# Splitting x of the first block part by part among the last steps of the first attention groups

## The chip, the cores and the metric

The kernel runs on one core of a Trainium2 chip. The metric is the time of one execution on the device, in microseconds (us). The engines are TensorE (PE: matmuls, and PEld: its weight loads), VectorE (DVE), ScalarE (ACT), GpSimd (POOL) and SyncE (SP), which issues the transfers.

## The reference

```
attention: q, k, v of (4, 8, 576, 64); causal, window of 64 keys
  scores = q k^T / sqrt(64), masked; softmax; times v
x = attention as (2304, 512)
FFN 1: g = x w_gate;  x1 = (silu(g) * (x w_val)) w_out      d_ff 1536
FFN 2: h = x1 w_in;   out = (h * clip(h + 3, 0, 6) / 6) w_out2   d_ff 2048
```

All arrays are float32 and are computed to about that precision: each matmul operand is split into a rounded upper part (`hi`) and the rest (`lo`), and a product is three matmuls, hi x hi, lo x hi and hi x lo.

## The kernel before, in words

The 2304 tokens are cut into blocks of 512, 512, 512, 384 and 384. Attention works in 36 groups of 256 tokens and two heads; `x` of a block of 512 tokens needs eight of them (two token groups by four head pairs). `x` is kept as four parts of 128 rows, `xr[:, kc]`, where part kc belongs to head pair kc.

`first_block()` (L506) computes the first eight groups alone, as nothing else can run yet. It is a pipeline written out by hand, one loop step s per group and six more to drain it: at step s it loads q and k of group s + 2 and `v` of group s - 1, stores the result of group s - 5 into `xr` (`store_x`, on ScalarE here), copies the transposed probabilities of group s - 4 out of PSUM (`evac_t`, L460, ScalarE for odd groups, VectorE for even ones), runs the two halves of the softmax for groups s - 1 and s - 2, then the matmuls: scores of group s (L403), transposes of group s - 3 (L452), values of group s - 4 (L471). At the end `pump(CONVERT_ATTENTION[s])` runs that many operations of the weight conversion.

The conversion `w_ops()` (L115) turns float64 weights into float32 on chip: per tile L129 and L134 (ScalarE), L148, L151, L186 and L192 (VectorE) rebuild the number, then L183 (ScalarE) takes the upper part and L199 (VectorE) the rest. A raw tile is loaded (L107) when L192 of an earlier one has been issued; five raw tiles are held. Tiles 3c, 3c + 1 and 3c + 2 are the gate, value and output weights of chunk c.

After `first_block`, `split_x` (L328) takes apart the four parts of `xr`: a cast on ScalarE into `xh` (L331) and a subtraction on VectorE into `xl` (L332). Then come 36 steps (block t, chunk c) of FFN 1, n = 0 to 35: the gate product (`gate`, L541 to L543, 12 matmuls of 128 x 512), tanh (L576) and L577 on it, the value product, L584, the split of the result (L564, L569) and the output product of the step before (L591 to L593). The groups of the next blocks and further conversion run among them.

What sets the order: inside a `tc.manual_schedule()` each engine runs its instructions in the order of the program. `first_block` is one such block of code, step n = 0 is another, and steps from n = 24 on a third. `split_x` and steps 1 to 23 stand outside of them; there a planner with a model of the chip's time orders each engine's instructions, and it also interleaves those with the ordered blocks and these with each other. In the trace, for example, ScalarE runs two conversion operations of step 0 ahead of the store of group 7.

`up` is the pool that holds `xh`, `xl` (four tags each), `u`, `uh` and `ul`; it is opened after `first_block` has closed its own pool `at`. Later code takes tiles of the tags `xh*` and `xl*` for other things (`wide_tile`, `ob` in `store_out`).

Of the kernel before, what the change touches and what calls it, by code (L numbers as in the profile page):

```python
# [11 lines left out]
F32 = mybir.dt.float32  # L12
F32R = mybir.dt.float32r
# [10 lines left out]
DM = H * D  # L24
# [4 lines left out]
KC = DM // 128  # L29
TB = 512  # L30
# [39 lines left out]
def attention_two_ffn(ctx: ExitStack, tc, qk, qq, v, w, out):  # L70
# [19 lines left out]
    def psum(tag, bufs=1):  # L90
        return ps.tile([128, 512], F32, tag=tag, name=tag, bufs=bufs)
# [17 lines left out]
    def load_ahead(n):  # L109

        while len(w_loaded) <= n + (4 if len(w_loaded) < NW1 else 3):
            w_loaded.append(len(w_loaded))
            w_load(w_loaded[-1])
# [101 lines left out]
    def pump(k):  # L215

        for _ in range(k):
            next(w_iter, None)
# [99 lines left out]
    xhl = {}  # L318

    def new_x():  # L320
        return xp.tile([128, KC, TB], F32, tag="xr", name="xr")
# [3 lines left out]
        nc.sync.dma_start(out=t[:, :, :src.shape[-1]], in_=src)  # L325
        return t

    def split_x(xr, kc, size):  # L328
        hi = up.tile([128, TB], F32R, tag=f"xh{kc}", name="xh", bufs=1)[:, :size]
        lo = up.tile([128, TB], F32R, tag=f"xl{kc}", name="xl", bufs=1)[:, :size]  # L330
        nc.scalar.copy(hi, xr[:, kc, :size])  # L331
        nc.vector.tensor_tensor(  # L332
            out=lo, in0=xr[:, kc, :size], in1=hi.bitcast(F32), op=ALU.subtract
        )
        xhl[kc] = (hi, lo)

# [3 lines left out]
    per_block = TB // GT * NPAIR  # L342
# [3 lines left out]
    def masks():  # L346
        nc.gpsimd.memset(mask, 0.0)
        for h in range(2):
            a = mask[64 * h:64 * h + 64, 0, :]
            nc.gpsimd.affine_select(  # L350
                out=a, in_=a, compare_op=ALU.is_ge, fill=MASKED / SCALE,
                base=-1, pattern=[[1, 128]], channel_multiplier=-1,
            )
            nc.gpsimd.affine_select(
                out=a, in_=a, compare_op=ALU.is_ge, fill=MASKED / SCALE,
                base=WIN, pattern=[[-1, 128]], channel_multiplier=1,
            )
        nc.gpsimd.memset(mask[0:64, 1, 0:64], MASKED / SCALE)
        nc.gpsimd.tensor_copy(mask[64:128, 1, 0:64], mask[64:128, 0, 0:64])
        nc.vector.tensor_copy(mask[:, 1, 64:128], mask[:, 0, 64:128])  # L360
        make_identity(nc, ident)

    def open_attention(stack, bufs):
        pool = stack.enter_context(tc.tile_pool(name="at", bufs=bufs["s"], side="right", reuse_waits="tile"))
        a_pool[:] = [pool, bufs]
# [30 lines left out]
    def quarter_scores(n, s):  # L396

        t = a_held.pop((n, "qk"))
        for u in range(GB):
            for h in range(2):  # L400
                rows = slice(h * D, (h + 1) * D)
                k0 = GT + u * WIN
                nc.tensor.matmul(  # L403
                    s[h][u % 2 * WIN:(u % 2 + 1) * WIN, u // 2 * 128:(u // 2 + 1) * 128],
                    t[rows, u * WIN:(u + 1) * WIN], t[rows, k0:k0 + 128],
                    start=True, stop=True,
                )
        a_held[n, "s"] = s
# [91 lines left out]
    def within(lo, hi):  # L500
        def at(fn, n, *more):
            if lo <= n < hi:
                fn(n, *more)
        return at

    def first_block():  # L506

        xr = new_x()
        with ExitStack() as st:
            bufs = {"qk": 3, "v": 4, "y": 4, "pt": 2, "s": 4, "xg": 0}  # L510
            open_attention(st, bufs)
            at = within(0, per_block)
            at(load_qk, 0)
            load_ahead(-4)
            at(load_qk, 1)
            load_ahead(1 - 4)
            masks()
            for s in range(per_block + 6):
                at(load_qk, s + 2)
                at(load_v, s - 1)  # L520
                if s in FIRST_LOADS:
                    load_ahead(2 + FIRST_LOADS.index(s) - 4)
                at(store_x, s - 5, xr)
                at(evac_t, s - 4)
                at(softmax_a, s - 1)
                at(softmax_b, s - 2)
                if s < per_block:
                    quarter_scores(s, [psum("acc", 4) for _ in "ab"] if s % 2 else [psum("g"), psum("c")])
                at(transposes, s - 3, "vd"[s % 2])
                at(values, s - 4, "acc", 4)  # L530
                pump(CONVERT_ATTENTION[s])
        return xr
# [29 lines left out]
    def u_hi(u):  # L562
        hi = up.tile([128, TB], F32R, tag="uh", name="uh")[:, :u.shape[-1]]
        nc.scalar.copy(hi, u)  # L564
        return hi
# [111 lines left out]
            )  # L677

    def wide_tile(k):
        return up.tile([128, TB], F32, tag=f"x{'hl'[k % 2]}{k // 2}", name="hw", bufs=1)  # L680

    sums = {}

    def wide_sums(c):
# [3 lines left out]
        if c == 0:  # L688
            t = new_x()
            fa, fb = t[:, 0, :], t[:, 1, :]  # L690
        else:
            fa, fb = wide_tile(6), wide_tile(7)
# [28 lines left out]
    def wide_chunk(c, out, between):  # L721
# [5 lines left out]
        def copy(k, a):  # L727
            t = wide_tile(k)[:, :TW]
            nc.scalar.copy(t, a)
            return t  # L730

        def plus(k, a, b):
            t = wide_tile(k)[:, :TW]
            nc.vector.tensor_tensor(out=t, in0=a, in1=b, op=ALU.add)
            return t
# [161 lines left out]
    def store_out(k):  # L897

        for a, r0 in done[:k]:
            n = r0 // 128 % 6  # L900
            ob = up.tile([128, DM], F32, tag=f"x{'hl'[n % 2]}{n // 2}", name="ob", bufs=1)
            if r0 == NT - 128:
                for h, q in enumerate((nc.sync, nc.scalar)):
                    half = slice(h * DM // 2, (h + 1) * DM // 2)
                    if h:
                        nc.scalar.activation(ob[:, half], a[:, half], AF.Copy, scale=1.0 / 6.0)
                    else:
                        nc.vector.tensor_scalar(
                            ob[:, half], a[:, half], 1.0 / 6.0, None, op0=ALU.mult
                        )  # L910
                    q.dma_start(out=out[r0:r0 + 128, half], in_=ob[:, half])
                continue
            if n % 2 and r0 >= NT - 2 * TH:
                nc.vector.tensor_scalar(ob, a, 1.0 / 6.0, None, op0=ALU.mult)
            else:
                nc.scalar.activation(ob, a, AF.Copy, scale=1.0 / 6.0)
            nc.sync.dma_start(out=out[r0:r0 + 128, :], in_=ob)
        del done[:k]
# [39 lines left out]
    def unit(i, before, others):  # L958
# [9 lines left out]
        if i == 0:  # L968
            for k in range(2):
                for _ in swish(ORDER[k], h[ORDER[k]]):  # L970
                    pass
            for k in range(2):
                split_g(ORDER[k], i)
            before()
            rest.append(chain(*(swish(k, h[k]) for k in ORDER[2:])))
        else:
            if i == 1:
                for k in ORDER[2:]:
                    split_g(k, 0)
            for m, name in enumerate(ORDER):  # L980
                ffn2_out(name, i - 1)
                if m % 2:
                    store_out(3)
                if m in (1, 2):
                    advance(others, 1)
                if now:
                    if m:
                        split_g(ORDER[m - 1], i)
                    for _ in swish(name, h[name]):
                        pass  # L990
            if now:
                rest.append(one(split_g, ORDER[-1], i))
# [14 lines left out]
            next(it, None)  # L1007

    with ExitStack() as fixed:
        with tc.manual_schedule():  # L1010
            xr = first_block()
        up = ctx.enter_context(tc.tile_pool(name="up", bufs=2, reuse_waits="tile"))
        for kc in range(KC):
            split_x(xr, kc, TB)
        st = ExitStack()
        open_attention(st, {"qk": 1, "v": 1, "y": 2, "pt": 1, "s": 3, "xg": 2})
        start = ExitStack()
# [2 lines left out]
        for n, (t, c) in enumerate(steps1):  # L1020
# [8 lines left out]
            def at(fn, step, *more):  # L1029
                if step in group_at:  # L1030
                    fn(group_at[step], *more)

            pumps = CONVERT[t] if t + 1 < NB or c < CONVERT_STOP else 0
            if t + 1 < NB and c == 1:
                xr = new_x()
# [8 lines left out]
            if last and t + 1 < NB:  # L1044
                for kc in range(KC):
                    split_x(xr, kc, SIZE[t + 1])
# [8 lines left out]
            hi = u_hi(u)  # L1055
# [89 lines left out]
        for i in range(NS * NU + 1):  # L1145
            s, n = divmod(i, NU)
# [70 lines left out]
```

## Time and profile before

| what | value |
|---|---|
| time, median of 3 runs | 924.49 us (924.35 to 925.01) |
| the profiled execution | 921.8 us, with a span of 920.0 us from the first to the last instruction |
| TensorE busy in the span | 893.4 us, 97% |
| VectorE busy | 701.9 us, 76% |
| ScalarE busy | 417.8 us, 45% |
| data moved by DMA | 207.52 MB, mean 226 GB/s |
| mean granted TensorE clock | 0.989 |

A timeline row gives the start and the busy time in us, the engine, the line of the kernel, the operation, the tile written and the tiles read, the shapes and the number of instructions put together; in square brackets stands how long the engine had idled before it and what released it. L12 is line 12 of the kernel. A row by stretch gives the stretch and its length, then the busy time and the number of instructions of PE, PEld, DVE, ACT and POOL, the granted share of TensorE's clock (1.00 is the 2.4 GHz level, 0.50 the 1.2 GHz level), the DMA engines' busy share and GB/s. A busy time reaches a little past the start of the next instruction, as the engines overlap the end of one with the next; so the distance from start to start is the price of one in a row of them.

### The profile page before, as it was taken

What the parts mean: (1) busy time and instruction counts of PE and PEld (TensorE: products, weight loads), DVE (VectorE), ACT (ScalarE), POOL (GpSimd) and SP (SyncE); (2) the same over time, 40 slices, a digit from 0 to 9 for tenths busy, and PEclk for the clock granted to TensorE, in tenths of its full rate; (3) what the DMA queues carried; (4) which work ended last, traced back from release to release, by engine and by line L of the source; (5) the groups of instructions that cost most, each with busy time, mean ns of one, the idle gap of its engine ahead of it and who ended that gap; (6) DMA issues with size and microseconds to landing.
All of it is one profiled execution on the core that took longest, in us unless ns stands there. A gap on an engine that the chain in (4) does not pass through costs nothing.

```text
span 920.0 us, 14498 instructions
## 1 busy us (share of the span) xinstructions
PE 893.4 (97%) x5088; PEld 781.3 (85%) x5088; DVE 701.9 (76%) x1629; ACT 417.8 (45%) x994; POOL 2.7 (0%) x14
## 2 busy tenths in 40 slices
PE   5799999999999999999999999999999999999998
PEld 3587778888877777889999999898989898989896
DVE  6899999988887778698888667767666767565654
ACT  6878888665776756344444432222132222211111
POOL 1000000000000000000000000000000000000000
PEclk8799999999999999999999999999999999999999
DMA  8557998778885978316545479765477565485601
GB/s 298 160 180 213 352 335 296 255 258 286 288 309 167 335 269 293 147 49 204 175 152 162 174 311 351 257 209 200 162 291 288 201 206 204 167 313 196 217 24 69
DMA packets 67608, 207.52 MB, mean 226 GB/s; under 512 B 7248, under 2 KB 14416, under 8 KB 67152
## 3 DMA queue, kind: packets, MB, share of 16 engines
q1 hardware_dynamic: 67392, 206.47, 64.5%
q8 instruction: 40, 0.66, 0.3%
q14 instruction: 32, 0.26, 0.1%
q10 hardware_dynamic: 144, 0.13, 0.0%
HBM read 157.16 MB, written 49.41 MB: 225 GB/s over the span
## 4 chain that ended last, share of the span: by engine, by line
PE 69%; DMA 12%; DVE 10%; ACT 6%; issue 2%; SPq 0%; ACTq 0%; DVEq 0%
DMA raw<-w_t 8%; PE acc L890 5%; PE acc L891 5%; PE acc L889 5%; PE v L848 3%; PE v L850 3%; PE v L849 3%; PE g L848 3%; PE g L850 3%; PE g L849 3%; PE acc L592 3%; PE acc L591 3%; PE acc L593 3%; DMA w2d<-ws 2%; DVE wf L186 2%
## 5 line engine op out<-in xcount | busy, mean ns | idle before, releaser
L869 ACT CAST gh<-g 128x384 fp32r<-128x384 f32 x96 | 49.3, 514 | 195.4 <-DVE g L860 170.9
L871 DVE TENSOR_TENSOR gl<-g,gh 128x384 fp32r<-128x384 f32 x96 | 53.3, 556 | 45.0 <-ACT gh L869 44.9
L592 PE MATMUL acc<-ul,wt 128*128 128x512 f32 (+1 forms) x216 | 81.6, 378 | 0.5 <-DVE ul L569 0.5
L593 PE MATMUL acc<-uh,wt 128*128 128x512 f32 (+1 forms) x216 | 80.4, 372 | 0.0
L891 PE MATMUL acc<-wt,gl 128*128 128x512 f32 x192 | 75.2, 391 | 0.0
L890 PE MATMUL acc<-wt,gh 128*128 128x512 f32 x192 | 75.1, 391 | 0.0
L889 PE MATMUL acc<-wt,gh 128*128 128x512 f32 x192 | 74.7, 389 | 0.0
L591 PE MATMUL acc<-uh,wt 128*128 128x512 f32 (+1 forms) x216 | 73.4, 373 | 0.4 <-ACT uh L564 0.4
L541 PE MATMUL g<-xh,wt 128*128 128x512 f32 x144 | 59.9, 416 | 3.6 <-ACT xh L331 2.4
L429 ACT ACTIVATE y<-y,s 128x128 f32<-128x128 f32 x144 | 56.3, 394 | 11.0 <-DVE s L423 10.8
L134 ACT ACTIVATE raw<-raw 128x512 int32<-128x512 uint32 x68 | 46.0, 677 | 33.2 <-DMA raw<-w_t 33.2
L542 PE MATMUL g<-xl,wt 128*128 128x512 f32 x144 | 57.4, 398 | 0.2 <-DVE xl L332 0.2
L541 PE MATMUL v<-xh,wt 128*128 128x512 f32 x144 | 57.3, 398 | 0.0
L543 PE MATMUL g<-xh,wt 128*128 128x512 f32 x144 | 57.1, 396 | 0.0
L848 PE MATMUL v<-xh,wt 128*128 128x384 f32 x168 | 56.7, 337 | 0.4 <-ACT q L935 0.4
L848 PE MATMUL g<-xh,wt 128*128 128x384 f32 x168 | 56.6, 337 | 0.0
L543 PE MATMUL v<-xh,wt 128*128 128x512 f32 x144 | 56.5, 393 | 0.0
L850 PE MATMUL v<-xh,wt 128*128 128x384 f32 x168 | 56.4, 336 | 0.0
L850 PE MATMUL g<-xh,wt 128*128 128x384 f32 x168 | 56.4, 336 | 0.0
L849 PE MATMUL v<-xl,wt 128*128 128x384 f32 x168 | 56.3, 335 | 0.0
L849 PE MATMUL g<-xl,wt 128*128 128x384 f32 x168 | 56.3, 335 | 0.0
L542 PE MATMUL v<-xl,wt 128*128 128x512 f32 x144 | 56.2, 390 | 0.0
(214 smaller groups left out, 2279.0 us busy)
## 6 DMA issues: line engine op xcount, KB each, us to landing
wt<-w2d SPq DMA_DIRECT2D x144, 512.0 KB, 4.9
raw<-w_t SPq DMA_DIRECT2D x68, 512.0 KB, 4.9
w2d<-ws SPq DMA_DIRECT2D x48, 512.0 KB, 4.5
wt<-w1d SPq DMA_DIRECT2D x33, 512.0 KB, 4.4
w1d<-wt SPq DMA_DIRECT2D x26, 512.0 KB, 5.5
v<-v_t SPq DMA_DIRECT2D x36, 256.0 KB, 4.6
qk<-qk_t SPq DMA_DIRECT2D x21, 416.0 KB, 5.3
x_out<-ob SPq DMA_DIRECT2D x17, 256.0 KB, 2.1
```

The costliest lines, as they stand in the source:

```text
L541: nc.tensor.matmul(dst, wt[:, 0, col], hi, start=kc == 0, stop=False)
L542: nc.tensor.matmul(dst, wt[:, 0, col], lo, start=False, stop=False)
L543: nc.tensor.matmul(dst, wt[:, 1, col], hi, start=False, stop=kc == KC - 1)
L591: nc.tensor.matmul(a, wt[:, 0, col], hi, start=c == 0, stop=False)
L592: nc.tensor.matmul(a, wt[:, 0, col], lo, start=False, stop=False)
L593: nc.tensor.matmul(a, wt[:, 1, col], hi, start=False, stop=c == NC1 - 1)
L848: nc.tensor.matmul(dst, wt[:, 0, col], hi[:, k, :], start=k == 0, stop=False)
L849: nc.tensor.matmul(dst, wt[:, 0, col], lo[:, k, :], start=False, stop=False)
L850: nc.tensor.matmul(dst, wt[:, 1, col], hi[:, k, :], start=False, stop=k == 1)
L889: nc.tensor.matmul(a, hi[:, row], wt[:, 0, :], start=begin, stop=False)
L890: nc.tensor.matmul(a, hi[:, row], wt[:, 1, :], start=False, stop=False)
L891: nc.tensor.matmul(a, lo[:, row], wt[:, 0, :], start=False, stop=end)
```

## The change

`split_x` is cut in two functions, `x_hi` (the cast) and `x_lo` (the subtraction). For the first block they are called in `first_block`: at step 9 + kc the cast of part kc, right behind the store that completes this part and ahead of `evac_t`; at step 10 + kc the subtraction, behind `evac_t`. They are part of the order written out by hand there. The tiles `xh` and `xl` come from a new pool `ux`, opened ahead of `first_block`, so that they don't lie where its tiles lie; `wide_tile` and `ob` take theirs from `ux` too. To make room, the first groups hold three tiles of `v` and of `y` in place of four, and `v` of a group is loaded one step later. The splits of later blocks stay where they were.

```diff
--- before.py
+++ after.py
@@ -325,14 +325,22 @@
         nc.sync.dma_start(out=t[:, :, :src.shape[-1]], in_=src)
         return t
 
-    def split_x(xr, kc, size):
-        hi = up.tile([128, TB], F32R, tag=f"xh{kc}", name="xh", bufs=1)[:, :size]
-        lo = up.tile([128, TB], F32R, tag=f"xl{kc}", name="xl", bufs=1)[:, :size]
+    def x_hi(xr, kc, size):
+        hi = ux.tile([128, TB], F32R, tag=f"xh{kc}", name="xh", bufs=1)[:, :size]
         nc.scalar.copy(hi, xr[:, kc, :size])
+        xhl[kc] = hi
+
+    def x_lo(xr, kc, size):
+        hi = xhl[kc]
+        lo = ux.tile([128, TB], F32R, tag=f"xl{kc}", name="xl", bufs=1)[:, :size]
         nc.vector.tensor_tensor(
             out=lo, in0=xr[:, kc, :size], in1=hi.bitcast(F32), op=ALU.subtract
         )
         xhl[kc] = (hi, lo)
+
+    def split_x(xr, kc, size):
+        x_hi(xr, kc, size)
+        x_lo(xr, kc, size)
 
 
 
@@ -507,7 +515,7 @@
 
         xr = new_x()
         with ExitStack() as st:
-            bufs = {"qk": 3, "v": 4, "y": 4, "pt": 2, "s": 4, "xg": 0}
+            bufs = {"qk": 3, "v": 3, "y": 3, "pt": 2, "s": 4, "xg": 0}
             open_attention(st, bufs)
             at = within(0, per_block)
             at(load_qk, 0)
@@ -517,11 +525,15 @@
             masks()
             for s in range(per_block + 6):
                 at(load_qk, s + 2)
-                at(load_v, s - 1)
+                at(load_v, s - 2)
                 if s in FIRST_LOADS:
                     load_ahead(2 + FIRST_LOADS.index(s) - 4)
                 at(store_x, s - 5, xr)
+                if per_block <= s - 1 < per_block + KC:
+                    x_hi(xr, s - 1 - per_block, TB)
                 at(evac_t, s - 4)
+                if per_block <= s - 2 < per_block + KC:
+                    x_lo(xr, s - 2 - per_block, TB)
                 at(softmax_a, s - 1)
                 at(softmax_b, s - 2)
                 if s < per_block:
@@ -677,7 +689,7 @@
             )
 
     def wide_tile(k):
-        return up.tile([128, TB], F32, tag=f"x{'hl'[k % 2]}{k // 2}", name="hw", bufs=1)
+        return ux.tile([128, TB], F32, tag=f"x{'hl'[k % 2]}{k // 2}", name="hw", bufs=1)
 
     sums = {}
 
@@ -898,7 +910,7 @@
 
         for a, r0 in done[:k]:
             n = r0 // 128 % 6
-            ob = up.tile([128, DM], F32, tag=f"x{'hl'[n % 2]}{n // 2}", name="ob", bufs=1)
+            ob = ux.tile([128, DM], F32, tag=f"x{'hl'[n % 2]}{n // 2}", name="ob", bufs=1)
             if r0 == NT - 128:
                 for h, q in enumerate((nc.sync, nc.scalar)):
                     half = slice(h * DM // 2, (h + 1) * DM // 2)
@@ -1007,11 +1019,10 @@
             next(it, None)
 
     with ExitStack() as fixed:
+        ux = ctx.enter_context(tc.tile_pool(name="ux", bufs=1, reuse_waits="tile"))
         with tc.manual_schedule():
             xr = first_block()
         up = ctx.enter_context(tc.tile_pool(name="up", bufs=2, reuse_waits="tile"))
-        for kc in range(KC):
-            split_x(xr, kc, TB)
         st = ExitStack()
         open_attention(st, {"qk": 1, "v": 1, "y": 2, "pt": 1, "s": 3, "xg": 2})
         start = ExitStack()
```

## Rows read from the trace of the kernel before

**Rows 1.** The page, engines' busy time and share of the span, whole run:

```profile
PE 893.4 (97%) x5088; PEld 781.3 (85%) x5088; DVE 701.9 (76%) x1629; ACT 417.8 (45%) x994; POOL 2.7 (0%) x14
```

**Rows 2.** Busy time by stretch (us, engines' busy time and instructions, clock, DMA share, GB/s):

```profile
0.00:23.00 23.00, 12.11 (x157) 8.97 (x157) 15.20 (x75) 14.42 (x54) 2.68 (x14) 0.85 0.86 298
...
46.00:170.00 124.00, 122.19 (x690) 98.84 (x689) 119.10 (x312) 102.31 (x256) 0.00 (x0) 1.00 0.79 269
...
250.00:920.00 670.00, 662.96 (x3617) 596.40 (x3615) 476.19 (x999) 229.60 (x497) 0.00 (x0) 1.00 0.60 211
```

**Rows 3.** Timeline of TensorE, 35 to 48 us:

```profile
35.96 1.12 PE L471 MATMUL acc<-pt,v 128*64 128x64 f32 x16 [0.96 <-ACT pt L460]
...
39.45 0.80 PE L541 MATMUL g<-xh,wt 128*128 128x512 f32 x1 [2.37 <-ACT xh L331]
...
41.98 0.80 PE L542 MATMUL g<-xl,wt 128*128 128x512 f32 x1 [0.16 <-DVE xl L332]
...
44.56 0.39 PE L541 MATMUL v<-xh,wt 128*128 128x512 f32 x1
...
47.31 0.39 PE L541 MATMUL g<-xh,wt 128*128 128x512 f32 x1
```

**Rows 4.** Timeline of ScalarE, 35 to 46 us:

```profile
35.05 0.37 ACT L483 COPY xr<-acc 128x256 f32<-128x256 f32 x1 [2.38 <-PE acc L471]
...
35.31 0.59 ACT L460 COPY pt<-v 128x512 f32<-128x512 f32 x1
...
38.77 1.66 ACT L331 CAST xh<-xr 128x512 fp32r<-128x512 f32 x3
...
44.44 0.66 ACT L134 ACTIVATE raw<-raw 128x512 int32<-128x512 uint32 x1 [1.77 <-DMA raw<-w_t]
...
45.00 0.58 ACT L576 ACTIVATE u<-g 128x512 f32<-128x512 f32 x1
```

**Rows 5.** Timeline of VectorE, 20 to 48 us:

```profile
20.94 0.69 DVE L460 COPY pt<-d 128x512 f32<-128x512 f32 x1 [1.91 <-PE d L452]
...
33.14 0.68 DVE L460 COPY pt<-d 128x512 f32<-128x512 f32 x1
...
40.03 0.69 DVE L192 CUSTOM_DVE_ANT_0 wf<-raw,wf 128x1024 uint16<-128x1024 uint16 x1
...
42.78 0.68 DVE L332 TENSOR_TENSOR xl<-xr,xh 128x512 fp32r<-128x512 f32 x1
...
43.38 0.42 DVE L151 TENSOR_SCALAR wf<-wf 128x512 uint32<-128x512 uint32 x1
...
45.61 0.69 DVE L577 SCALAR_TENSOR_TENSOR u<-u,g 128x512 f32<-128x512 f32 x1 [1.81 <-ACT u L576]
...
47.54 0.69 DVE L199 TENSOR_TENSOR wt<-wf,wt 128x512 fp32r<-128x512 f32 x1
```

**Rows 6.** Busy time by stretch around the rise of the clock, columns as in rows 2:

```profile
36.60:39.90 3.30, 0.94 (x11) 0.58 (x7) 2.80 (x6) 3.30 (x8) 0.00 (x0) 0.50 0.61 186
40.00:43.30 3.30, 3.14 (x7) 1.96 (x7) 3.30 (x7) 2.67 (x5) 0.00 (x0) 0.50 0.45 114
43.40:46.00 2.60, 2.60 (x13) 2.11 (x12) 0.79 (x3) 1.56 (x4) 0.00 (x0) 1.00 0.11 44
```

**Rows 7.** Score matmuls of group 5, loads of `v` before 30 us, the page's row:

```profile
18.63 1.23 PE L403 MATMUL acc<-qk 64*64 64x128 f32 x16 [4.13 <-DMA qk<-qq_t]
...
DMA to landing us min/median/max: 2.6/5.1/8.6
...
v<-v_t SPq DMA_DIRECT2D x36, 256.0 KB, 4.6
```

**Rows 8.** Timeline around weight tile 9, and TensorE's wait near 100 us:

```profile
64.86 0.69 DVE L199 TENSOR_TENSOR wt<-wf,wt 128x512 fp32r<-128x512 f32 x1
...
66.20 0.50 PE L541 MATMUL g<-xh,wt 128*128 128x512 f32 x1
...
99.88 0.50 PE L541 MATMUL g<-xh,wt 128*128 128x512 f32 x1 [1.17 <-DVE u L577]
```

## The prediction

> **What bounds the kernel now.** I read the stages first [rows 1, 2]. From 46 us to the end TensorE is the bound: 122.19 of 124 us busy between 46 and 170, 662.96 of 670 from 250 on. VectorE is nearly as full in the first of these stretches (119.10 of 124), because it converts the weights there. So a microsecond taken from the time before 46 us ends up in the total only if VectorE, too, comes that much earlier; after 170 us TensorE has the longer day alone and carries whatever lead it has.
>
> Then the hand-over from the first eight attention groups to the FFN, engine by engine. TensorE ends the values of group 7 at 37.08 (35.96 + 1.12) and starts the first gate product at 39.45, having idled 2.37 us for `xh` [rows 3]. The twelve products then take 39.45 to 44.56, that is 5.11 us, of which 0.16 is one wait for `xl`; the rest is 0.41 us each. The pace is a matter of the clock: it is granted at half (0.50, the 1.2 GHz level) until 43.3 and in full from 43.4 [rows 6]. After that a product comes every 0.23 us (twelve from 44.56 to 47.31) [rows 3]. On ScalarE the store of group 7 and the four casts of `x` stand behind conversion work; the first three casts run at 38.77 to 40.43 [rows 4]. VectorE is busy without a longer pause from 20.94 to 43.80, then waits 1.81 us for the tanh of chunk 0, which needs those products [rows 5].
>
> **The change part by part.**
>
> *Casts and subtractions moved.* No work is added: four casts of some 0.55 us of ScalarE's time (1.66 / 3) and four subtractions of 0.60 (42.78 to 43.38). Casts 0 and 1 now come at steps 9 and 10. Cast 1 fits in the 2.38 us for which ScalarE idles before 35.05, so it costs nothing; without that cover it would be 0.55 on ScalarE. Cast 0 stands in front of the copy of `pt` of group 5 and moves the values of group 5 by 0.55; what follows on TensorE there is paced by VectorE, which doesn't wait for it. Cast 2 stands between the store of group 6 (35.05) and the copy of `pt` of group 7 (35.31, 0.59), for which TensorE waits already [rows 3, 4]. So values 7 start at 36.5 and end at 37.6. This 0.55 is the price on the path.
>
> *TensorE's start.* Parts 0 to 2 are split by then, so the first product needs nothing but the engine: 37.6 in place of 39.45, and the 0.16 wait goes. Gain 2.37 - 0.55 + 0.16 = 1.98. Part 3 comes last: store 7 at 37.7, cast 3 to 38.5, subtraction 3 on VectorE at 39.3 to 39.9 (below). Nine products at 0.41 keep TensorE until 41.3, so it isn't waited for.
>
> *The clock.* In before it rose 3.9 us after the restart at 39.45, with only 0.16 us idle in between [rows 3, 6]. Now values 7 and the products follow each other from 36.5. Counted from there, the rise falls at 40.4, and half speed covers 2.8 us of products in place of 3.9: a further (3.9 - 2.8) / 2 = 0.55. The other end is that the rise stays at 43.4: then half speed covers 5.8 us and (5.8 - 3.9) / 2 = 0.95 is lost. If it comes as early as 40.0, 0.8 is won. I take 0.55, as the work ahead of the rise is as dense as in before. So 12 products end 1.98 + 0.55 = 2.5 us sooner, at 42.0.
>
> The Trainium skill, "TensorE: Matmul & The Clock Gate", section "What's actually happening", speaks against taking a fixed delay: what decides "doesn't reset when your kernel starts", so that the point of the rise varies. No run here shows that yet; by it the clock term is any value between the two ends just given, and the sum 1.0 to 2.8 us.
>
> *VectorE.* Does it follow? From 33.14 its order becomes: copy 6, subtraction 0, `wt` 1, two steps of a conversion, subtraction 1, and so on, subtraction 3 at about 39.3. The work up to 43.80 is the same and only some 0.6 us of small waits go, so it is through at about 43.1. Then tanh 0 is done (products at 42.0, tanh 0.6), and L577 runs at 43.1 in place of 45.61: VectorE gains 2.5 too. Inside, conversions come later at first: L192 of raw tile 5 at 40.03 [rows 5] moves behind all four subtractions, to about 40.85. Weight tile 4 follows three operations after L577: 47.54 becomes 45.1, done at 45.7, and TensorE asks for it two chunks of twelve later, at 42.0 + 24 x 0.23 = 47.5.
>
> The tightest weight that I found later is tile 9: VectorE starts its last subtraction at 64.86 (done at 65.55) and TensorE uses it at 66.20, 0.65 us later [rows 8]. So TensorE may gain at most what VectorE gains plus 0.65, that is 3.1; 2.5 is inside.
>
> *`v` one step later, with three buffers.* A later load of `v` has the same release: with three buffers and one step of delay it waits for the same values matmuls as before. In the crowded beginning it changes the order of transfers: `v` 0 leaves the way of qk 5, for which TensorE stood 4.13 us until 18.63 [rows 7]. 256 KB at the 298 GB/s of that stretch [rows 2, 7] are 0.9 us. What starts there reaches VectorE at 20.94, after a wait of 1.91, and VectorE is full from then on, so up to 0.9 us could be won; none if the transfers ahead have slack. On the loss side `v` lands 2.6 to 8.6 us after its issue [rows 7]; issued a step later, `v` 0 to 2 land just ahead of their use, and a late one is paid on the same path, up to some 0.5 us. I take +0.3, between -0.5 and +0.9.
>
> The Trainium skill, "Trainium Kernel Development and Optimization", section "Best Practices", asks for double buffering so that transfers overlap compute; by that rule a cut is a risk. Three buffers with the same release are still more than two; by it the term would be at worst the -0.5 above.
>
> *`y` with three buffers.* The wait is for transposes that stand just behind the scores which the same softmax needs, and at even steps VectorE's copy of `pt` waits for them anyhow (the 1.91 at 20.94). Zero; if that cover were missing, a transpose group, about 1 us.
>
> *The pool of their own.* wide_tile and ob only change the pool. Zero; no row shows a wait of theirs that decides.
>
> **Sum.** 1.98 + 0.55 + 0.3 = 2.8 us on TensorE, with VectorE at 2.5 + 0.3. Against the profiled execution: 920.0 - 2.8 = 917.2 of span, 919.0 of 921.8 with what lies around it. That execution lies 2.7 us below the median of the timed runs, 924.49; I take the same difference off the median: 921.7. A bonus not counted: TensorE idles 0.96 us ahead of values 7, and products of part 0 could be placed there, as the orders written out by hand in different blocks are interleaved by the planner (up to 0.6 more).
>
> **The rivals.**
>
> *The tanh stays behind a load.* ScalarE ran a conversion step of a later raw tile (L134) ahead of tanh 0 and waited 1.77 us for its transfer, to 44.44; tanh came at 45.00 [rows 4]. That transfer is issued when L192 at 40.03 is done, which I place 0.8 us later. If the planner keeps this order, tanh 0 comes at about 45.6, L577 at 46.3, weight tile 4 is done 0.7 later than before, at 48.9; TensorE used it at about 44.56 + 24 x 0.23 = 50.1, so it now waits and keeps a gain of 1.2 at most, less what the other tiles lack (up to 1.0). For it: the order in before is like that. Against it: the planner puts first what it expects first, and the products now come earlier. Time 923.3 to 924.3.
>
> *The clock rises no earlier.* Then 1.98 - 0.95 + 0.3 = 1.3: 923.2. For: the products' pace in before was all half clock. Against: the work ahead of it is denser now. This is the case that the skill's page allows.
>
> *Products fill the idle time.* With the part 0 products ahead of values 7, and the larger load term, up to 2.5 + 0.6 + 0.9 = 4.0, held by VectorE to about 2.5 + 0.9 + 0.65 = 4.05: 920.5.
>
> *A new order of the conversions, the slower end.* Steps 1 to 23 are ordered by the planner, not by hand, and a moved start gives it another picture. A conversion is five VectorE operations, some 2.6 us; if tile 9 came one conversion later, TensorE would wait 2.6 - 0.65 = 1.95 there. At 99.88 such a delay stands already: 1.17 us for L577 [rows 8]. One of them leaves a gain of 0.9; from two on (3.9 us against 2.8) the kernel is slower, with three it is at 924.5 - 2.8 + 5.85 = 927.5. Against it: the order of tiles and the budget of operations per step are the same in both kernels.
>
> **How the numbers follow.** A measurement of this kernel can tell about 0.2% from no change, 1.85 us. Forecast with the fill case: 0.60 (0.44 and 0.16), both faster than 922.6. Tanh behind the load: 0.14. Clock: 0.12, both within 0.2%. New order: 0.14, of which 0.04 ends within 0.2% and 0.10 slower. So faster 0.60, same 0.30, slower 0.10. The range: from 920.2, the fill case with a little rounding, to 924.8, which takes in the clock and the tanh rivals and leaves out the slower end and part of the fill case.
>
> **What would show it.** Right: in the changed profile the first gate product starts at about 37 to 37.6 with no wait for `xh`, L577 of chunk 0 comes near 43 with no long wait, the idle of TensorE between 23 and 46 falls by some 2 us, and its busy time after 46 stays. Each step by its row: qk 5's wait (18.63) shorter by up to 0.9, values 7 at 36 to 36.5, the clock in full near 40, tile 4 done near 45.5. Wrong: a first product at 39 or later; ScalarE still waiting for a raw tile ahead of tanh 0; new waits of TensorE for L577 or `wt` between 46 and 170; a wait for `v` in the first 25 us.

## The result and the profile after

The changed kernel takes 927.38 us (median), the kernel before 922.75 us in the same comparison: a ratio of 1.0061, 95% interval 1.0047 to 1.0075. It is slower by 0.6%, where 921.7 us and "faster" had been forecast. (The forecast, a gain of 2.8 us, started from the median of three runs, 924.49; the kernel before has 922.75 over the 20 runs of this comparison, so 1.7 us of the distance to 921.7 belong to that starting point.) Executions of one kernel spread here over some 6 us (the kernel before: 919.04 to 925.01), and a profile shows one of them. So sizes are taken from the ratios below, and the traces are read for the place of a loss.

| | before | after |
|---|---|---|
| the profiled execution, span | 921.8, 920.0 us | 927.0, 925.2 us |
| TensorE busy in the span | 893.4 us | 896.6 us |
| ScalarE's idle time ahead of L134, waiting for raw tiles | 33.2 us | 41.8 us |

In the changed code the lines have moved: the products are L553 to L555 (gate and value), tanh is L588, L577 has become L589 and L584 has become L596; the cast of `x` is L330, the subtraction L336; scores L398, transposes L460, copies of `pt` L468, values L479, stores L491. L449 scales the probabilities `y` of a group on ScalarE.

The hand-over first. TensorE's timeline from the changed kernel (answering [rows 3]); the `acc` row at 35.65 is the values of group 7:

```profile
29.55 0.50 PE L553 MATMUL g<-xh,wt 128*128 128x512 f32 x1 [0.27 <-ACT xh L330]
...
35.65 1.12 PE L479 MATMUL acc<-pt,v 128*64 128x64 f32 x16
36.70 0.80 PE L554 MATMUL g<-xl,wt 128*128 128x512 f32 x1
...
40.50 0.48 PE L553 MATMUL v<-xh,wt 128*128 128x512 f32 x1
...
43.88 0.50 PE L553 MATMUL g<-xh,wt 128*128 128x512 f32 x1 [0.37 <-DVE u L589]
```

The planner put gate products into TensorE's idle time from 29.55 on, the values of group 7 follow with no wait, and the twelve gate products are through where the value products begin, at 40.50, not at 44.56. VectorE and ScalarE of the changed kernel (answering [rows 4, 5]):

```profile
40.63 0.69 DVE L192 CUSTOM_DVE_ANT_0 wf<-raw,wf 128x1024 uint16<-128x1024 uint16 x1
...
43.14 0.69 DVE L589 SCALAR_TENSOR_TENSOR u<-u,g 128x512 f32<-128x512 f32 x1 [0.42 <-ACT u L588]
...
45.08 0.68 DVE L199 TENSOR_TENSOR wt<-wf,wt 128x512 fp32r<-128x512 f32 x1
```

```profile
42.53 0.58 ACT L588 ACTIVATE u<-g 128x512 f32<-128x512 f32 x1
```

L589 comes 2.5 us earlier than L577 did, weight tile 4 is done 2.5 us earlier. Up to here it is the picture forecast. Now the stretches (columns as in [rows 2]), of the kernel before and then of the changed one:

```profile
23.00:46.00 23.00, 16.14 (x154) 11.81 (x152) 20.18 (x54) 18.58 (x53) 0.00 (x0) 0.70 0.51 160
46.00:70.00 24.00, 24.00 (x128) 19.49 (x127) 23.40 (x62) 18.71 (x47) 0.00 (x0) 1.00 0.59 183
...
110.00:140.00 30.00, 30.00 (x182) 23.96 (x181) 29.06 (x81) 26.37 (x69) 0.00 (x0) 1.00 0.96 336
140.00:170.00 30.00, 29.79 (x159) 24.57 (x159) 29.35 (x76) 23.17 (x54) 0.00 (x0) 1.00 0.74 260
170.00:250.00 80.00, 80.00 (x479) 65.28 (x478) 71.19 (x192) 52.92 (x140) 0.00 (x0) 1.00 0.82 282
```

```profile
23.00:46.00 23.00, 19.55 (x161) 14.16 (x158) 21.55 (x56) 18.86 (x48) 0.00 (x0) 0.76 0.50 160
46.00:70.00 24.00, 22.22 (x121) 17.84 (x121) 23.40 (x63) 20.82 (x53) 0.00 (x0) 1.00 0.60 188
...
110.00:140.00 30.00, 28.28 (x173) 22.37 (x171) 26.57 (x73) 25.03 (x68) 0.00 (x0) 1.00 0.96 333
140.00:170.00 30.00, 28.11 (x161) 22.27 (x161) 29.30 (x80) 22.42 (x58) 0.00 (x0) 1.00 0.70 242
170.00:250.00 80.00, 76.24 (x448) 62.30 (x447) 67.53 (x182) 51.09 (x132) 0.00 (x0) 0.99 0.83 277
```

In the first of them TensorE idles 3.45 us (23 - 19.55), half of before. In those from 46 to 70 and 110 to 250 it idles 9.15 us (1.78 + 1.72 + 1.89 + 3.76), where before it idled 0.21. In some other stretches it idles less than before; over all the time from 46 us to the end it is 15.6 us against 8.9, and 3.3 us from about 248.9 on run at the half clock level, which costs another 1.6. That is 8.4 us lost, against some 3.2 won ahead of 46: the 5.2 by which the span grew. TensorE's larger waits in the stretches shown, in the changed kernel:

```profile
55.33 0.46 PE L398 MATMUL c<-qk 128*128 128x128 f32 x2 [1.38 <-DMA qk<-qk_t]
139.77 0.33 PE L460 MATMUL d<-ident,y 128*128 128x128 f32 x1 [1.66 <-ACT y L449]
152.47 0.49 PE L398 MATMUL c<-qk 128*128 128x128 f32 x2 [1.32 <-DMA qk<-qk_t]
165.60 0.50 PE L554 MATMUL g<-xl,wt 128*128 128x512 f32 x1 [0.57 <-DVE xl L336]
224.17 0.44 PE L460 MATMUL d<-ident,y 128*128 128x128 f32 x2 [1.28 <-ACT xr L491]
247.31 0.50 PE L553 MATMUL g<-xh,wt 128*128 128x512 f32 x1 [1.38 <-DVE u L589]
249.09 0.48 PE L460 MATMUL d<-ident,y 128*128 128x128 f32 x1 [0.82 <-ACT xr L491]
```

None of these has to do with the first block's `x`. They belong to attention groups and chunks that come 10 to 200 us later, and the work is the same; what differs is the order in which the planner has put it. Compared place by place, some 300 of ScalarE's 854 instructions in the program are others than before, and some 900 of TensorE's 4599 (the count depends a little on what is taken as the same instruction). One wait traced back, ahead of 139.77, on ScalarE and VectorE of the changed kernel:

```profile
136.41 0.68 ACT L134 ACTIVATE raw<-raw 128x512 int32<-128x512 uint32 x1 [2.31 <-DMA raw<-w_t]
...
139.33 1.27 ACT L449 ACTIVATE y<-y,s 128x128 f32<-128x128 f32 x4
```

```profile
137.90 0.69 DVE L199 TENSOR_TENSOR wt<-wf,wt 128x512 fp32r<-128x512 f32 x1 [2.66 <-ACT wt L183]
```

ScalarE waits 2.31 us for a raw tile's transfer. Behind that L134 stand a cast for VectorE's L199, which therefore waits 2.66, and L449, for whose `y` TensorE's transposes wait.

### The profile page after: what moved, and what is told of

The parts are those of the page before. It is cut to its first block, busy times and chain, and to the rows that moved or that the text cites. A ratio compares the mean times of both kernels' runs of the same rounds, so it can differ in the third digit from the quotient of the medians.

```text
span 925.2 us, 14505 instructions
## 1 busy us (share of the span) xinstructions
PE 896.6 (97%) x5088; PEld 783.3 (85%) x5088; DVE 702.0 (76%) x1629; ACT 419.2 (45%) x994; POOL 2.7 (0%) x14
## 4 chain that ended last, share of the span: by engine, by line
PE 65%; DVE 1%; ACT 1%; issue 0%; ACTq 0%; DVEq 0%
PE acc L902 5%; PE acc L903 5%; PE acc L901 5%; PE v L860 3%; PE v L862 3%; PE v L861 3%; PE g L860 3%; PE g L862 3%; PE g L861 3%; PE acc L604 2%; PE acc L605 2%; PE acc L603 2%; PE d L903 1%; PE d L902 1%; PE c L902 1%; PE d L901 1%
## 5 line engine op out<-in xcount | busy, mean ns | idle before, releaser
L134 ACT ACTIVATE raw<-raw 128x512 int32<-128x512 uint32 x68 | 45.9, 676 | 42.0 <-DMA raw<-w_t 41.8
L553 PE MATMUL g<-xh,wt 128*128 128x512 f32 x144 | 60.8, 422 | 2.3 <-DVE u L589 2.1
L555 PE MATMUL g<-xh,wt 128*128 128x512 f32 x144 | 58.0, 403 | 0.0
L553 PE MATMUL v<-xh,wt 128*128 128x512 f32 x144 | 57.2, 397 | 0.5 <-DVE u L596 0.4
L555 PE MATMUL v<-xh,wt 128*128 128x512 f32 x144 | 56.6, 393 | 0.0
L576 ACT CAST uh<-u 128x512 fp32r<-128x512 f32 (+1 forms) x48 | 28.4, 592 | 61.7 <-DVE u L596 32.3
```

The source lines that it names most:

```text
L553: nc.tensor.matmul(dst, wt[:, 0, col], hi, start=kc == 0, stop=False)
L555: nc.tensor.matmul(dst, wt[:, 1, col], hi, start=False, stop=kc == KC - 1)
```

## Experiments

For most of them the first 34 steps were written out: every instruction up to there is collected first and then issued from one list for each engine, so the planner orders none of them. All lines of that part show L176, the helper's.

```diff
+    nc = _Recorder(tc.nc, ORDER, SLOTS)
+    ctx.enter_context(tc.manual_schedule())
...
-        with tc.manual_schedule():
-            xr = first_block()
+        xr = first_block()
```

In the lists below `raw.10` is L134 of raw tile 10, `wf.7` L129 of tile 7, `wt.4` the cast for weight tile 4, `u.0` tanh 0, `xr` a store, `xh.3` the cast of part 3.

**Controls.** `r_before` issues the order of the kernel before from such a list, `r_after` that of the changed kernel.

> The kernel before with every engine's order written out: the first 34 steps are issued in the very order that the planner had given each engine in the kernel before. It is the control of the method. Both theories: 1.000 of the kernel before, within 0.2%.

> The changed kernel with every engine's order written out, as the planner had given it. Control. Both theories: 1.006 of the kernel before (1.0047 to 1.0075), as the changed kernel measured.

Measured: 1.0009 (0.9995 to 1.0022) and 1.0057 (1.0039 to 1.0074). Writing an order out costs nothing that can be told, and the changed kernel's loss comes back with its order written out. So its order can now be exchanged by itself.

**The order alone, and the head alone.** `r_order_new` keeps the head of before (the splits behind the first groups) and takes the changed kernel's order behind it. `r_head_new` has the split part by part, `v` a step later and the smaller buffers, and the order of before behind it. ScalarE's list of `r_head_new` against `r_before`:

```diff
-xr pt.5 wf.4 wt.1 xr raw.4 xr pt.7 wf.5 wt.2 wt.3 raw.6 xr raw.5 xh.0 xh.1 xh.2 wf.6 xh.3
+xr xh.0 pt.5 wf.4 wt.1 xr xh.1 raw.4 xr xh.2 pt.7 wf.5 wt.2 wt.3 raw.6 xr xh.3 raw.5 wf.6
 raw.9 wf.7 raw.10 u.0 wt.4 raw.7
```

> The first block as in the kernel before (split behind it, four buffers), with the order of the steps behind it as the planner chose it for the changed kernel; the products of step 0 stand behind the last values matmuls again. Theory A: the loss stays and the head's gain is gone, ratio 1.006 to 1.011. Theory B: no loss, 0.998 to 1.002.

> The changed first block (splits among its last steps, operands in their own pool, three buffers of v and y, v one step later), with the order of the steps behind it as in the kernel before. Theory A, the loss is the order that the planner chose for steps 1 to 23: the head keeps its gain of about 3 us and nothing is lost, ratio 0.997 (0.9955 to 0.9985). Theory B, the loss is physical (an earlier start meets raw tiles that come no earlier, or three buffers and the pool cost waits): the kernel loses again, ratio 1.002 to 1.008.

Measured: `r_order_new` 934.54 us, 1.0137 (1.0118 to 1.0155), slower even than the changed kernel; its waits at 59.82 (1.36, `qk`), 143.48 (1.76, `y`), 157.10 (2.23, `qk`) and 228.05 (1.44, `xr`) are those of the changed kernel some 4 us later. That is above the 1.006 to 1.011 expected: with this order the new head is worth 0.8% (1.0137 against 1.0057 of `r_after`), with the order of before, as the next runs show, next to nothing. Why the two differ so stays open. `r_head_new` 924.17 us, 1.0030 (1.0017 to 1.0044): the gain that was expected from the head isn't there, and the time lies in the range of theory B, though of those waits only one, for `xr` at 252.47 (1.34), comes back. Most of what it lost stands in one place. ScalarE, VectorE and TensorE of `r_head_new`:

```profile
44.94 0.65 ACT L176 ACTIVATE raw<-raw 128x512 int32<-128x512 uint32 x1 [2.29 <-DMA raw<-w_t]
45.50 0.58 ACT L176 ACTIVATE u<-g 128x512 f32<-128x512 f32 x1
```

```profile
46.10 0.69 DVE L176 SCALAR_TENSOR_TENSOR u<-u,g 128x512 f32<-128x512 f32 x1 [3.38 <-ACT u L176]
```

```profile
46.85 0.50 PE L176 MATMUL g<-xh,wt 128*128 128x512 f32 x1 [2.24 <-DVE u L176]
```

`raw.10` waits for its transfer ahead of tanh 0: the first rival of the prediction.

**One ScalarE instruction moved, in two steps.** `r_tanh_first` puts tanh 0 ahead of `raw.10`; `r_cast_first` puts `raw.10` behind `wt.4` and `raw.7` too, which is the changed kernel's own order there.

```diff
-raw.9 wf.7 raw.10 u.0 wt.4 raw.7
+raw.9 wf.7 u.0 raw.10 wt.4 raw.7      (r_tanh_first)
+raw.9 wf.7 u.0 wt.4 raw.7 raw.10      (r_cast_first)
```

> The new first block with the old order behind it, and one instruction moved: on ScalarE the tanh of chunk 0 goes ahead of the conversion step of raw tile 10, which waited 2.29 us for its transfer and held the tanh back, so that VectorE waited 3.38 us and TensorE 2.24. Theory C, the loss of the new head with the old order is this one wait and the clock's fall behind it: the gain of the head comes out, ratio 0.997 (0.9955 to 0.9985). Theory B, an earlier start is met by later waits wherever it meets them: within 0.999 to 1.003.

> The new head of the changed kernel, then the order of before, with tanh 0 ahead of L134 of raw tile 10 on ScalarE (as in r_tanh_first), and that L134 now also behind the cast of weight tile 4 and one conversion step of raw tile 7. In r_tanh_first this L134 waited 1.78 us (to 45.01) for its transfer, held the cast of weight tile 4, and TensorE waited 1.41 us at 48.45. Theory A (the split itself gains; what is lost are a few ScalarE instructions that stand behind a load which now comes too late): the wait of 1.41 falls below 0.5, and the time is 0.997 of before, between 0.995 and 0.999. Rival B (VectorE's work bounds the start anyhow, so that TensorE gives back any lead by 60 us): a wait of the same size stands a little later, before 70 us, and the time is within 0.998 to 1.002.

Measured: 1.0000 (0.9983 to 1.0018) and 0.9996 (0.9982 to 1.0010). In the first, L577 comes at 43.26, but `raw.10` now holds `wt.4`, and TensorE waits 1.41 at 48.45; in the second that wait is gone and no wait above 0.25 stands between 40 and 250 us. The first step wins back the 0.3% that `r_head_new` had lost, not the further 0.3% that were expected; the second adds nothing that can be told from the noise. TensorE of `r_cast_first`, and its stretches around the clock's rise:

```profile
36.37 1.12 PE L176 MATMUL acc<-pt,v 128*64 128x64 f32 x16 [1.61 <-ACT pt L176]
37.42 0.80 PE L176 MATMUL g<-xh,wt 128*128 128x512 f32 x1
...
42.55 0.40 PE L176 MATMUL v<-xh,wt 128*128 128x512 f32 x1
```

```profile
36.00:42.00 6.00, 5.63 (x27) 4.56 (x28) 5.39 (x11) 5.23 (x10) 0.00 (x0) 0.50 0.48 137
42.40:46.00 3.60, 3.60 (x18) 2.96 (x17) 3.10 (x7) 2.55 (x5) 0.00 (x0) 1.00 0.52 146
```

**Products of part 0 ahead of the values of group 7.** `r_fill` is `r_tanh_first` with them, `r_cast_fill` is `r_cast_first` with them. On TensorE:

```diff
-values 7, gate part 0 (hi hi, lo hi, hi lo), gate part 1
+gate part 0 (hi hi, lo hi, hi lo), values 7, gate part 1
```

> As the kernel with tanh 0 first, and on TensorE the three products of part 0 stand ahead of the values of group 7. If TensorE's start decides, some 0.6 us more is gained, ratio about 0.7 thousandths lower; if VectorE's full queue decides when chunk 0 goes on, the same ratio within 0.3 thousandths.

> r_cast_first with three gate products of part 0 placed ahead of the values of group 7 on TensorE, as the planner of the changed kernel had placed them. Theory A: another 0.3 to 0.6 us, 0.9965 of before, between 0.994 and 0.998. Rival B (VectorE bounds): the same time as r_cast_first within 0.0005, TensorE waiting longer for VectorE by what the fill gained.

Measured: 0.9992 (0.9972 to 1.0011) and 0.9987 (0.9970 to 1.0005). TensorE waits 0.93 us for VectorE at 43.60 in `r_cast_fill`, so VectorE takes back much of what the fill wins; the intervals don't tell the two accounts apart. `r_cast_fill` is the best version found; that it beats the kernel before is not shown. But it settles the cause of the loss: it has the code, the pools and the numbers of buffers of `r_after`, and differs from it only in the order written out (and in which buffer a tile takes, which follows from the order): 0.9987 against 1.0057.

**Parts of the change, left to the planner.** `p_buffers` makes only the buffers smaller and loads `v` later. `p_split` makes only the split and its pool (`v` keeps four buffers, `y` has three).

```diff
-            bufs = {"qk": 3, "v": 4, "y": 4, "pt": 2, "s": 4, "xg": 0}
+            bufs = {"qk": 3, "v": 3, "y": 3, "pt": 2, "s": 4, "xg": 0}      (p_buffers)
+            bufs = {"qk": 3, "v": 4, "y": 3, "pt": 2, "s": 4, "xg": 0}      (p_split)
```

> Only the buffers: three of v and y, v one step later; the split stays behind the first block. The planner gives every engine the same order as before but for the first loads on SyncE, so this is the cost of the buffers alone. Prediction: a gain of 0.3 us, between a loss of 0.5 and a gain of 0.9: ratio 0.9997 (0.999 to 1.0005). If a late v or y holds the first block: 1.001 or more.

> Only the split moved into the first block, with the pool of its own, four buffers of v and no later load (y has three to make room), ordered by the planner. Theory A, the order chosen for steps 1 to 23 loses more than the head gains: 1.003 to 1.010. If the buffers were the loss: 0.997.

Measured: 0.9996 (0.9978 to 1.0014) and 1.0070 (1.0047 to 1.0093). The buffers are free and leave the planner's order as it was (only the first loads differ). The split brings the new order, and with it the loss: the orders of ScalarE, VectorE and TensorE in `p_split` are those of the changed kernel, instruction by instruction.

**Other orders by the planner.** `p_null_order` is the kernel before, `p_after_order` the changed kernel, each with step 0 no longer held in its written order.

```diff
             if n == 0:
-                start.enter_context(tc.manual_schedule())
+                pass
```

> The kernel before, with one line changed: step 0 of the FFN is no longer held in the written order, so that the planner places it, and all steps to 23, anew. Work, buffers and the place of the splits are those of before. Theory A (a new order by the planner is by itself worth several tenths of a per cent either way, and this is what the changed kernel lost): the time differs from before by more than 0.2 per cent, between 0.99 and 1.02, more likely slower, with new waits of TensorE of 0.5 to 2 us each between 46 and 250 us. Rival B (the planner's orders are about equal, and the loss belongs to the moved split): within 0.2 per cent, no more than two such waits.

> The changed kernel with the same one line changed: step 0 is not held in the written order, so that the planner orders the steps to 23 anew with the split in the first groups. Theory A (order is a draw): it differs from the changed kernel's 1.006 by more than 0.002, either way, between 0.99 and 1.02. Rival B (the split costs whatever the order): 1.004 to 1.008, with the waits for qk near 55 and 153 us and for raw tiles on ScalarE as in the changed kernel.

Measured: 1.0046 (1.0029 to 1.0063) and 1.0076 (1.0062 to 1.0090). The first has the work, the buffers and the splits of before: a new order alone costs 0.5%; its profile has five waits of 0.5 to 1.4 us between 46 and 250 us. The second hits the time that was expected if the split costs by itself, but not the places: the waits for `qk` near 55 and 153 are gone, the idle time ahead of L134 is 29.0 us against 42.0, and the loss stands behind step 24, where the written order begins again: it is 2.6 us ahead of the kernel before at step 24 and 7.3 behind at step 25. TensorE is busy for 3.45 of the 10 us from 290 to 300. TensorE of `p_null_order`, then of `p_after_order`:

```profile
37.64 0.58 PE L390 MATMUL c<-qk 128*128 128x128 f32 x1 [1.20 <-DMA qk<-qk_t]
...
49.37 0.33 PE L452 MATMUL d<-ident,y 128*128 128x128 f32 x1 [1.42 <-ACT y L441]
```

```profile
44.95 0.58 PE L398 MATMUL c<-qk 128*128 128x128 f32 x1 [2.67 <-DVE s L431]
...
299.42 0.45 PE L460 MATMUL v<-ident,y 128*128 128x128 f32 x1 [4.68 <-DVE u L596]
```

**Which stretch of the new order.** `r_new_until_12` takes the changed kernel's order up to a gate product and that of `r_cast_fill` from there on; `r_new_from_12` the other way round. The names and the expectations call it the first product of step 12, but it is that of step 8: TensorE's list in `r_new_until_12` leaves the changed kernel's after 96 gate products, which is eight steps of twelve. Step 8 begins at 117 us in the changed kernel (the "about 110 us" of the expectation), step 12 only at 162 us. In short:

```diff
-order = [*CAST_FILL]
+order = [*AFTER[:c], *(i for i in CAST_FILL if i not in AFTER[:c])]      (r_new_until_12)
+order = [*CAST_FILL[:c], *(i for i in AFTER if i not in CAST_FILL[:c])]  (r_new_from_12)
```

> The changed kernel's order written out until the first gate product of step 12 (about 110 us), then the order of before as in r_cast_fill. r_cast_fill (new head, then the order of before) was at 0.9987 and the changed kernel at 1.0061; the question is where the 0.0074 between them lie. Theory A (spread over the order, each stretch loses by waits of its own): in the profile of the changed kernel the lead at step 12 was 4.6 us smaller than in r_cast_fill (1.8 late against 2.8 early), 8.7 us at step 24 and 7.2 at the end; so this kernel loses something like half, 0.002 to 0.005, and stands at 1.001 to 1.004, with the wait for qk near 55 us and none for qk near 153 or for xr near 224. Rival B (it is all behind step 12): 0.998 to 1.000. Rival C (the early order takes the raw tiles in a way that is paid for later, whatever the order then): 1.005 to 1.008.

> The counterpart: r_cast_fill's order (new head, then that of before) until the first gate product of step 12, then the order of the changed kernel. Theory A (spread): the rest of the loss, 1.002 to 1.005, with the waits near 140 (transposes for y), 153 (scores for qk) and 224 (transposes for xr) and none for qk near 55; the losses of the two kernels add up to about 0.0074. Rival B (all behind step 12): 1.005 to 1.008. Rival C (all ahead of it): 0.998 to 1.000.

Measured: 1.0035 (1.0018 to 1.0051) and 1.0131 (1.0105 to 1.0157). The first is where a loss spread over the order should be, the second beyond all three accounts. Against `r_cast_fill` the two lose 0.0048 and 0.0144, together more than twice the 0.0074 of the whole order: losses of parts don't add up, and an order joined from two has a price of its own. How far the single profiles stand from that of the kernel before when step n begins (its second gate product; us, minus is earlier):

| kernel | n = 2 | 6 | 8 | 12 | 22 | end |
|---|---|---|---|---|---|---|
| after | -0.3 | -2.6 | -3.9 | +1.8 | +8.6 | +5.2 |
| `r_after` | +0.1 | -2.2 | -3.5 | +1.7 | +10.2 | +7.4 |
| `p_split` | +2.0 | -0.4 | -1.8 | +5.2 | +11.5 | +8.9 |
| `r_order_new` | +4.2 | +1.4 | +0.1 | +6.4 | +12.3 | +9.9 |
| `r_new_from_12` | -0.9 | -1.3 | -1.3 | +2.6 | +11.7 | +12.8 |
| `r_new_until_12` | -0.5 | -2.9 | -2.9 | -2.1 | -2.3 | +1.5 |
| `r_cast_fill` | -2.8 | -3.7 | -3.7 | -2.8 | -1.6 | -2.0 |
| `r_before` | -1.4 | -2.1 | -2.1 | -1.0 | +0.5 | 0.0 |

Every kernel with the changed kernel's order behind step 8 falls back by 12 to 14 us between steps 8 and 22, whatever its head; the three with the order of before in that stretch by 0.6 to 2.6, `r_new_until_12` among them. In `r_new_from_12` the waits at 153.31 (1.28, `qk`) and one of 2.57 for `pt` at 219.66 are in that stretch. At step 8 the changed kernel is still level with `r_cast_fill`. So in the profiles the loss is made by the order of steps 8 to 22, and where nothing is joined some 3 us of it are won back behind them. The time of `r_new_until_12` says that the part ahead of step 8 isn't free either, or that the join isn't; its profiled execution, at 923.25 its fastest, loses some 2.4 us behind step 31, with a wait of 1.45 at 367.04. `r_new_from_12` has the same wait at 378.26 (1.45), the kernels that aren't joined don't have it. Where the other executions of `r_new_until_12` lose, and why the other join costs 6 us more than the changed kernel itself, stays open.

## Why the prediction was wrong

**What bounds the kernel** was read rightly: TensorE's idle time after 46 us went straight into the total. But "its busy time after 46 stays" was the step that failed: the sum took the steps behind the first block as they were. In their place the runs show a new order of steps 1 to 23, in which TensorE idles 15.6 us after 46 (8.9 before) and loses 1.6 more by the clock, against some 3.2 won ahead of 46; with that order taken out the loss is gone (`r_after` 1.0057, `r_cast_fill` 0.9987).

**TensorE's start** held. Without the fill, `r_cast_first` starts the values of group 7 at 36.37 and the first gate product at 37.42 (36.5 and 37.6 forecast); `r_head_new` and `r_tanh_first`, with the same head, are 0.6 to 0.7 us earlier. The price on the path, 0.55, was 0.65: TensorE waits 1.61 us ahead of these values in all three, where it had waited 0.96. The waits for parts of `x` among the products were larger than the 0.16 read: the first seven products took 3.96 us in the kernel before (39.45 to 43.41), all at half level, and 3.15 in `r_cast_first` (37.42 to 40.57), at half level too. So the 0.41 us read as the pace of a product is the mean of two levels and of these waits. In the changed kernel the case of products in the idle time came true as well.

**The clock** came out by chance. The full level began between 40.6 and 40.7 in the changed kernel (40.4 forecast), but between 42.0 and 42.4 in `r_cast_first`, whose first product started where it was forecast; so half level covered 5 us of its products and not 2.8, and the twelve ended at 42.55 and not at 42.0. Stretches of the changed kernel (answering [rows 6]), then of `r_cast_fill`:

```profile
38.00:40.60 2.60, 2.60 (x7) 1.60 (x7) 2.15 (x5) 1.81 (x4) 0.00 (x0) 0.50 0.82 296
40.70:43.30 2.60, 2.60 (x12) 1.95 (x11) 2.14 (x5) 2.04 (x4) 0.00 (x0) 1.00 0.38 74
```

```profile
33.00:35.90 2.90, 2.87 (x29) 1.94 (x27) 2.77 (x6) 2.05 (x5) 0.00 (x0) 0.50 0.58 215
36.30:39.00 2.70, 2.29 (x11) 1.24 (x9) 2.43 (x5) 2.67 (x7) 0.00 (x0) 0.99 0.58 154
```

With nearly the same work the full level began near 36 us in `r_cast_fill` and at 40.7 in the changed kernel; with the same head and the same order of TensorE it began near 41.4 (`r_head_new`), 39.5 (`r_tanh_first`) and 42.3 us (`r_cast_first`). So the term should have kept its whole width in the sum. This agrees with the Trainium skill, "TensorE: Matmul & The Clock Gate", section "What's actually happening", by which the gate's timing "doesn't reset when your kernel starts".

**VectorE follows** held to 0.2 us: L577 at 43.14 (43.1), L192 at 40.63 (40.85), tile 4 at 45.08 (45.1).

**`v` and the buffers**: 0.9996 measured, 0.9997 forecast (0.3 us), but the interval takes in the whole range given, so only a larger effect is excluded. The row that was to show it can't: the wait for qk 5 ends at 17.84 in `p_buffers` and at 18.63 in the kernel before, but at 17.61 in `r_before`, which has the buffers and loads of before.

**The sum**, 2.8 us, was too large even with the old order kept: `r_cast_first` gains 0.4 us (0.0004 x 922; from a gain of 1.7 to a loss of 0.9), `r_cast_fill` 1.2 (a gain of 2.8 to a loss of 0.5). The step behind it, that what TensorE and VectorE gain by 46 us reaches the end, is not safe: `r_before` was 2.1 us early at step 6 and level at the end, having lost the lead in waits such as 1.11 at 97.80 and 0.89 for a weight tile at 139.61. That this is also what swallowed the head's gain in the timed runs is argued, not shown: `r_cast_first` and `r_cast_fill` keep 2.4 and 2.0 us of lead to the end of their profiles, but `p_buffers`, without the new head, ends 3.3 us early, so single profiles don't decide it.

**The rival of tanh behind a load** was the right reading of before's order: `r_head_new` has tanh at 45.50 (45.6) and L577 at 46.10 (46.3). Its 924.17 us lie within the 923.3 to 924.3 given only by luck: that range was a gain of 0.2 to 1.2 us on 924.49, and in this comparison the kernel before has 921.81, so that `r_head_new` loses (1.0030). In the changed kernel itself the planner put tanh first, as the argument against the rival had said.

**The rival of a new order** is what happened, and its chance of 0.14, 0.10 of it slower, was the mistake. The argument against it, that "the order of tiles and the budget of operations per step are the same in both kernels", is true and decides nothing: the planner places ScalarE's and TensorE's instructions freely within that, and a conversion step that waits for a load ahead of a softmax or a tanh is enough. The mechanism in it did not come: it made a weight tile late by one conversion, and none of TensorE's larger waits is for a weight tile; they are for loads of `qk`, for `y`, `pt`, `xl`, for stores into `xr` and for L589. The signs named for "wrong" were therefore mostly not those that came. The size of one was near, waits of 0.6 to 1.7 us against 1.95 each, but there were eight of them between 55 and 250 us (the seven shown and 0.67 for `pt` at 86.53), in stretches that had been taken as unchanged; that three late conversions had given 927.5 us, and 927.38 was measured, is luck. No row of before could have shown the new order, but that steps 1 to 23 are ordered anew was known, and the three new orders measured here (the changed kernel's, `p_null_order`'s and `p_after_order`'s) cost 0.5% to 0.8%.

## What to carry to other kernels

Where a planner orders a part of the kernel, a change to what stands ahead of that part is two changes: the local one, whose places in time the profile told well here, though not what of it reaches the end, and a fresh order of everything behind, which it doesn't price at all; the second was a loss in the three cases here (in one of them only where the planned part ends). Write the old order out and issue it behind the new head before judging the head. In an order by hand, look first for instructions that wait for a load and stand ahead of work the bounding engine needs: here moving one of them on ScalarE was worth 0.3%.

## What the runs showed of the hardware

A wait of TensorE can cost a second time by the clock, and its length doesn't tell whether it will. In `r_head_new` the 2.24 us at 46.85 were followed by half level from about 48.2 to 51.6:

```profile
48.30:51.50 3.20, 3.20 (x9) 2.46 (x9) 3.03 (x7) 2.02 (x4) 0.00 (x0) 0.50 0.72 213
51.70:54.00 2.30, 2.30 (x11) 1.90 (x11) 2.30 (x6) 2.30 (x6) 0.00 (x0) 1.00 0.76 237
```

In the changed kernel half level came with the waits at 247.31 and 249.09 too (1.38 and 0.82 us), from 248.9 to 252.3, some 1.6 us of loss (3.3 us at half pace), while the 1.66 us at 139.77 were followed by none:

```profile
249.00:252.20 3.20, 3.11 (x10) 2.63 (x11) 3.19 (x6) 2.21 (x5) 0.00 (x0) 0.50 0.71 274
...
139.70:143.00 3.30, 3.23 (x15) 2.58 (x16) 3.30 (x8) 2.79 (x8) 0.00 (x0) 1.00 1.01 407
```

Two waits as long as the one in `r_head_new` were followed by none either: in `r_order_new` the granted clock stays at 1.00 from 154.5 to 164 us, in `r_new_from_12` from 217 to 228:

```profile
157.10 0.38 PE L176 MATMUL c<-qk 128*128 128x128 f32 x1 [2.23 <-DMA qk<-qk_t]
```

```profile
219.66 0.34 PE L176 MATMUL d<-pt,v 128*64 128x64 f32 x4 [2.57 <-ACT pt L176]
```
